# Three 512-column spin matmuls become 52 of 64 columns in the opening of a retention and Mish-MLP kernel

## The chip, the core and the metric

The kernel runs on one core of one Trainium2 chip. The metric is the device time of one execution, in microseconds (us). A core has a matrix engine (TensorE, "PE" in the profile; its weight loads are listed apart as "PEld"), a vector engine (VectorE, "DVE"), a scalar engine (ScalarE, "ACT"), GpSimd ("POOL") and SyncE ("SP"), which here only issues DMAs. Each engine works through its own list of instructions in order and waits on semaphores for the others.

## What is computed

A linear recurrence with decay (retention) over 4 batches, 8 heads, 768 steps and 64 channels, followed by a two-layer network over the 3072 tokens:

```python
for t in range(S):
    state = gamma * state + einsum('bhd,bhe->bhde', k[:, :, t], v[:, :, t])
    y[:, :, t] = scale * einsum('bhd,bhde->bhe', q[:, :, t], state)
x = y.transpose(0, 2, 1, 3).reshape(B * S, H * D)     # 3072 x 512
h = x @ w_in                                          # 512 x 2048
g = h * tanh(log1p(exp(h)))                           # Mish
out = g @ w_out                                       # 2048 x 512
```

Inputs and output are float32; the matrix work is done in float16 with float32 sums.

## The kernel before

The steps are cut into chunks of 128 (`C`). Within a chunk the outputs come from a masked matrix of scores (q times k, lower triangle) times v; across chunks a 64x64 state per head is carried. Chunks are gathered into blocks: the first block has four, the others two each (`BLOCKS`). For a block, the kernel makes the retention output transposed (`xt`), multiplies it by `w_in` (lines 687, 818, 1055), applies Mish on ScalarE, multiplies by `w_out` (lines 954, 1207, 1267) and stores. From the second block on, both products are done with seven half-size products in place of eight, which is where the many sums on VectorE come from. The order of instructions is written out by hand (`tc.manual_schedule()`); no scheduler moves them.

The change lies in `first_block`, before any data has arrived. SyncE issues the loads of the first 512 steps of q (`load_first_q`, tile `qfirst`), then of k and v, then of the weights. While they travel, GpSimd writes two constants, the identity `ident` (float16) and the triangle `tri` (float32), and TensorE runs matmuls whose result nobody reads ("spins"). There are two kinds: `spin_wide` (line 457) multiplies `tri` by copies of itself in float32, `n` times 128 columns, which the hardware does in two records of one instruction; `spin` (line 452) multiplies `ident` by copies of itself in float16, 512 columns a matmul. All write into the first score tile `at`, which the first scores overwrite later. In front of the first transpose stand two wide spins of 512 columns (`HP` is 4) and `spin(at, 8)`, two matmuls of 512 columns.

What follows on TensorE, in order: the transposes of the first half of q (line 264, eight of 128 columns, in `turn_first_q`), which need q scaled by VectorE (line 257); a wide spin of 128 columns; the eight transposes of the second half, whose input VectorE and GpSimd share; the transposes of k (line 307, `turn_two`), four for each half of the heads; a wide spin of 128; the scores (line 322). ScalarE copies the first transposed q out (line 272) and the transposed k (line 312); VectorE casts k (line 291), copies the second transposed q (line 274) and then masks the scores (line 329). The state sums (lines 341, 351, 353), the outputs (lines 382, 389) and the first product with `w_in` (line 1055) follow.

Of the kernel before, what the change touches and what calls it, by code (L numbers as in the profile page):

```python
# [16 lines left out]
def kernel(  # L17
# [9 lines left out]
    nc = tc.nc  # L27
# [6 lines left out]
    HP = H // 2  # L34
# [3 lines left out]
    HB = P // R  # L38
# [45 lines left out]
    ident = cpool.tile([P, P], FP16, name="ident")  # L84
# [158 lines left out]
    def load_first_q():  # L243

        qf = wstage.tile([P, H, CPB, D], FP32, name="qfirst", tag="wt", bufs=4)
        for a in range(0, H, H // 2):
            nc.sync.dma_start(
                qf[:, a:a + H // 2],
                q[0, a:a + H // 2, :TB].rearrange("h (p r) d -> p h r d", r=CPB))
        return qf  # L250

    def turn_first_q(qf, half, shared=False):
        a, n = half * (H // 2), H // 2
        q16 = castp.tile([P, CPB, n, D], FP16, name="qfirst16", bufs=1, tag=f"qfirst16_{half}")
        m = n // 2 if shared else n
        for b in range(0, n, m):
            (nc.gpsimd if b else nc.vector).tensor_tensor(
                q16[:, :, b:b + m].rearrange("p r h d -> p h r d"), qf[:, a + b:a + b + m],
                qs_spread[:, a + b:a + b + m].unsqueeze(3).broadcast_to((P, m, CPB, D)),
                op=ALU.mult)  # L260
        t_ps = mmps.tile([P, n // 2, CPB, P], FP16, name="t_ps", tag="mm")
        for i in range(n // 2):
            for r in range(CPB):
                nc.tensor.transpose(t_ps[:, i, r], q16[:, r, 2 * i:2 * i + 2], ident)  # L264
        return t_ps

    def first_q_out(half, t_ps, eng):
        n = HP // 2
        dst = qfirst_t[:, half * n:(half + 1) * n].rearrange("p i (t r) -> p i t r", r=CPB)
        src = t_ps.rearrange("p i r t -> p i t r")  # L270
        if eng is nc.scalar:
            nc.scalar.copy(dst, src)
        else:
            eng.tensor_copy(dst, src)

    def load_two(nm, s, half):
        t = lpool.tile([P, HP, R, D], FP32, name=nm + "f", tag=nm + "f", bufs=6 if nm == "v" else 4)
        nc.sync.dma_start(
            t, dict(k=k, v=v)[nm][
                0, half * HP:(half + 1) * HP, s * R * P:(s + 1) * R * P].rearrange(  # L280
                "h (p r) d -> p h r d", r=R))
        raw[nm, s, half] = t

    def cast_two(nm, s, half, by_vector=False):
        src = raw.pop((nm, s, half))
        if nm == "k":
            if s not in k16s:
                k16s[s] = castp.tile([P, 2, R, HP, D], FP16, name="qk16")
            dst = k16s[s][:, half].rearrange("p r h d -> p h r d")
            if by_vector:  # L290
                nc.vector.tensor_copy(dst, src)
            else:
                nc.scalar.copy(dst, src)
        else:
            v16s[s, half] = castp.tile([P, R, HP, D], FP16, name="v16")
            nc.gpsimd.tensor_tensor(
                v16s[s, half].rearrange("p r h d -> p h r d"), src,
                vs_two[:, half * HP:(half + 1) * HP].unsqueeze(3).broadcast_to((P, HP, R, D)),
                op=ALU.mult)
# [10 lines left out]
    def turned_two(s, half):  # L310
        n = HP // 2
        nc.scalar.copy(kts[s][:, half * n:(half + 1) * n], t16s.pop((s, half)))
# [133 lines left out]
    def at_tile():  # L446
        return atps.tile([P, 2, HP // 2, R, C], FP32, name="at", tag="at")

    def spin(at, n):
        for i in range(0, n, HP):  # L450
            m = min(HP, n - i)
            nc.tensor.matmul(
                at[:, 0].rearrange("p j r t -> p (j r) t")[:, :m], ident,
                ident.unsqueeze(1).broadcast_to((P, m, P)), start=True, stop=True)

    def spin_wide(at, n):
        nc.tensor.matmul(  # L457
            at[:, 0].rearrange("p j r t -> p (j r) t")[:, :n], tri,
            tri.unsqueeze(1).broadcast_to((P, n, C)), start=True, stop=True)
# [570 lines left out]
    def load_weights():  # L1030
        for s in range(NSL):
            load_w("in", s)
        for s in range(NSL):
            load_w("out", s)
        room(CPB)
        room(CPB + 1)
        load_one(CPB, 0, nc.sync)
        load_one(CPB, 2, nc.sync)
        load_one(CPB + 1, 0, nc.sync)
# [19 lines left out]
    def first_block():  # L1059
        qf = load_first_q()  # L1060
        for s in range(2):
            for nm in "kv":
                for half in range(2):
                    load_two(nm, s, half)
        nload[0] = CPB
        load_weights()
        xts[0] = xtp.tile([P, CPB, HP, C], FP16, name="xt")

        at = at_tile()
        spin_wide(at, HP)  # L1070
        spin_wide(at, HP)
        spin(at, 8)
        tq = turn_first_q(qf, 0)
        spin_wide(at, 1)
        first_q_out(0, tq, nc.scalar)
        tq = [tq, turn_first_q(qf, 1, True)]
        cast_two("k", 0, 0, True)
        turn_two(0, 0)
        turned_two(0, 0)
        cast_two("k", 0, 1, True)  # L1080
        turn_two(0, 1)
        first_q_out(1, tq[1], nc.vector)
        turned_two(0, 1)
        spin_wide(at, 1)
        scores_half(0, 0, at)
        mask_half(0, 0, at)
        for half in range(2):
            cast_two("v", 0, half)
        at = at_tile()
        spin_wide(at, 1)  # L1090
        scores_half(0, 1, at)
        mask_half(0, 1, at)
        cast_two("k", 1, 0)
        turn_two(1, 0)
        turned_two(1, 0)
        cast_two("k", 1, 1)
        outer_first(0)
        state_first(0)
        at = at_tile()
        scores_half(1, 0, at)  # L1100
        mask_half(1, 0, at)
        y = atps.tile([P, 2, HP, C], FP32, name="y_ps", tag="at")
        in_two = [y[:, c] for c in range(2)]
        present_first(0, in_two, range(HP))
        turn_two(1, 1)
        turned_two(1, 1)
        state_first(1)
        past_first(1, in_two)
        xt_out(0, y)
        for half in range(2):  # L1110
            cast_two("v", 1, half)
        cast_win(0, 0, nc.gpsimd)
        at = at_tile()
        scores_half(1, 1, at)
        mask_half(1, 1, at)
        y = [atps.tile([P, 2, HP, C], FP32, name="y_ps", tag="at")[:, 0] for _ in range(2)]
        outer_first(1, [0])
        state_first(2)
        h_ps = [mmps.tile([P, 1, TB], FP32, name="h_ps", tag="mm") for _ in range(2)]
        for u in range(2):  # L1120
            first_g1(h_ps[u], u, 0)
        present_first(1, y, range(HP))
        past_first(2, y)
        past_first(3, y)
        cast_win(0, 1, nc.vector)
        xt_out_by_two(2, y)
        for u in range(2, FPS):
            h_ps.append(mmps.tile([P, 1, TB], FP32, name="h_ps", tag="mm"))
            first_g1(h_ps[u], u, 0)
        for u in range(FPS):  # L1130
            first_g1(h_ps[u], u, 1)
            mish(0, u, h_ps[u])
        for s in range(1, NSL - 1):
            for half in range(2):
                cast_win(s, half, nc.vector)
            if s == 1:
                fourth_state()
            if s == 2:
                late.extend(win_sums(0))
                some_late(8)  # L1140
        room_for_sums()

        def more_sums():
            late.extend(win_sums(1))
            some_late(8)
            late.extend(weight_sums(0) + weight_sums(1))

        plan = {6: [(cast_win, NSL - 1, 0, nc.scalar)],
                7: [(cast_win, NSL - 1, 1, nc.scalar), (more_sums,)],
                9: [(cast_wout, 0, 1), (room_for_more,), (bring_first,)],  # L1150
                10: [(some_late, 1)],
                12: [(g_sum, 1)],
                13: [(cast_wout, 1, 2), (room_for_more,), (g_sum, 2), (g_sum, 3)],
                16: [(load_more,)]}
        for u in range(FPS, NFB):
            g1(0, u)
            for fn, *args in plan.get(u + 1, ()):
                fn(*args)
        first_g2()
        hsnaps.append(gp.tile([P, 4, TB], FP32, name="hsnap", tag="g0"))  # L1160
# [251 lines left out]
```

## Time and profile before

| | us |
|---|---|
| three timed runs | 192.44, 192.24, 191.39 |
| their median | 192.24 |
| the profiled execution | 191.71 |
| its span, first to last instruction | 189.8 |
| TensorE busy in it | 183.3 |
| VectorE, ScalarE, GpSimd busy in it | 156.7, 126.0, 94.7 |

The profile is one execution recorded by the hardware. Its span is shorter than its time, since start and end of the program lie around it. In its rows, "128x512 f32" is partitions by elements; "x8" counts instructions; "L264" is line 264 of the kernel. "[0.25 <-PE t_ps L264]" says that the engine had been idle for 0.25 us and what ended that. A merged row of the timeline gives the first start and the time covered, not the duration of one instruction. The end of a matmul is modelled, so the record of one overlaps the next; steps between starts are the better measure. The chain of waits starts at the last instruction and goes back, at each step, to what released it or to the instruction before it on its engine.

### The profile page before, as it was taken

The numbers are of one execution on the slowest core, as the hardware profiler recorded it, in microseconds if no ns is written. First come the engines' busy times: TensorE is split into PE (matmuls) and PEld (weight loads), VectorE is DVE, ScalarE is ACT, GpSimd is POOL, SyncE is SP. The second block draws the span as 40 slices with busy tenths as digits, with TensorE's granted clock in tenths as the row PEclk, the third lists the DMA queues.
The fourth block names the chain that finished last, engine by engine and source line by source line (L and its number), as shares of the span: only waits on it lengthen the run. The fifth ranks groups of instructions, "written<-read, shape, count | busy, mean of one in ns | idle before, by whom it ended". The sixth has DMA issues, their size and how long they took to land.

```text
span 189.8 us, 7746 instructions
## 1 busy us (share of the span) xinstructions
PE 183.3 (97%) x3298; PEld 156.9 (83%) x3298; DVE 156.7 (83%) x330; ACT 126.0 (66%) x244; POOL 94.7 (50%) x135
## 2 busy tenths in 40 slices
PE   6989999999999999999999999999999999999992
PEld 2667546875988988988988988988988988989981
DVE  3997899889899698797897897797897897796662
ACT  3362699463893983894883883983884974975960
POOL 6570205696767937934934935915925923000000
PEclk9999999999999999999999999999999999999999
DMA  4999999999999999999996996996997953300203
GB/s 165 351 369 406 405 406 279 269 217 147 186 195 281 193 264 217 175 192 170 176 184 148 159 176 196 207 233 40 196 205 106 155 152 60 114 3 12 102 0 111
DMA packets 95521, 36.17 MB, mean 191 GB/s; under 512 B 82560, under 2 KB 88960, under 8 KB 95488
## 3 DMA queue, kind: packets, MB, share of 16 engines
q1 hardware_dynamic: 74112, 32.78, 73.7%
q0 software_dynamic: 21088, 2.62, 21.7%
q8 instruction: 25, 0.41, 0.9%
q10 hardware_dynamic: 288, 0.30, 0.4%
q14 instruction: 8, 0.07, 0.1%
HBM read 27.30 MB, written 6.29 MB: 177 GB/s over the span
## 4 chain that ended last, share of the span: by engine, by line
PE 94%; DVE 3%; issue 1%; POOL 0%; ACT 0%; POOLq 0%; DVEq 0%
PE h_ps L818 34%; PE o_ps L954 32%; PE h_ps L687 6%; PE o_ps L1207 5%; PE at L457 2%; PE h_ps L1055 2%; PE o_ps L1267 2%; PE y_ps L542 2%; PE at L509 2%; PE u_ps L495 2%; DVE am L329 2%; PE y_ps L553 2%; PE t_ps L264 1%; DVE osb L975 1%; PE at L322 0%
## 5 line engine op out<-in xcount | busy, mean ns | idle before, releaser
L838 DVE TENSOR_TENSOR hsum<-h_ps,hsnap 128x512 f32<-128x512 f32 x60 | 38.6, 685 | 9.7 <-ACT hsnap L828 6.8
L828 ACT COPY hsnap<-h_ps 128x512 f32<-128x512 f32 x60 | 32.1, 589 | 10.0 <-PE h_ps L818 9.7
L818 PEld LDWEIGHTS <-wsum 128*128 128x128 f16 x640 | 36.2, 98 | 0.2
L833 ACT ACTIVATE g<-hsum 128x512 f16<-128x512 f32 x60 | 34.6, 642 | 0.6 <-DVE hsum L838 0.2
L954 PEld LDWEIGHTS <-gsum 128*128 128x128 f16 x320 | 30.4, 98 | 3.7
L818 PE MATMUL h_ps<-xsum,wsum 128*128 128x128 f16 x480 | 30.2, 219 | 0.0
L954 PE MATMUL o_ps<-tmat,gsum 128*128 128x256 f16 x240 | 29.5, 273 | 0.0
L818 PEld LDWEIGHTS <-win 128*128 128x128 f16 x480 | 28.2, 98 | 0.9
L426 POOL DMA_DIRECT2D qk<-in_k_dram x36 | 27.6, 781 | 0.0
L954 PEld LDWEIGHTS <-g 128*128 128x128 f16 x248 | 22.7, 98 | 2.5
L414 POOL TENSOR_TENSOR qk<-qf,qvs 128x512 f16<-128x512 f32 x20 | 21.5, 1077 | 0.2 <-issue 0.2
L431 POOL TENSOR_TENSOR v<-vf,qvs 128x512 f16<-128x512 f32 x20 | 21.2, 1085 | 0.0
L954 PE MATMUL o_ps<-wout,g 128*128 128x256 f16 (+1 forms) x168 | 20.8, 267 | 0.0
L818 PE MATMUL h_ps<-xt,win 128*128 128x128 f16 x320 | 19.6, 219 | 0.0
L603 POOL TENSOR_TENSOR stc<-suc,gcv 128x256 f16<-128x256 f32 x15 | 9.9, 663 | 15.7 <-DVE suc L598 15.7
L560 ACT COPY hsum<-y_ps 128x512 f32<-128x512 f32 x9 | 5.3, 585 | 18.4 <-PE y_ps L553 18.4
L975 DVE TENSOR_TENSOR osb<-o_ps,snap 128x256 f32<-128x256 f32 (+1 forms) x32 | 13.0, 413 | 5.0 <-PE o_ps L954 2.5
L439 POOL COPY gate<-gsum 128x1 f16<-128x1 f16 x10 | 1.8, 185 | 26.8 <-DVE gsum L925 26.8
L963 ACT COPY snap<-o_ps 128x256 f32<-128x256 f32 x31 | 11.4, 371 | 5.5 <-PE o_ps L954 5.3
L818 PE MATMUL h_ps<-xsum,win 128*128 128x128 f16 x160 | 12.3, 220 | 0.0
L818 PE MATMUL h_ps<-xt,wsum 128*128 128x128 f16 x160 | 12.2, 219 | 0.0
L833 ACT ACTIVATE g<-h_ps 128x512 f16<-128x512 f32 x20 | 12.0, 598 | 0.0
(142 smaller groups left out, 310.6 us busy)
## 6 DMA issues: line engine op xcount, KB each, us to landing
vf<-in_v_dram SPq DMA_DIRECT2D x24, 256.0 KB, 6.0
out_dram<-osb SPq DMA_DIRECT2D x22, 256.0 KB, 3.5
qf<-in_q_dram SPq DMA_DIRECT2D x20, 256.0 KB, 4.9
wi<-in_moe_w_in_dram SPq DMA_DIRECT2D x3, 1024.0 KB, 10.5
wt<-in_moe_w_out_dram SPq DMA_DIRECT2D x3, 1024.0 KB, 9.3
qk<-in_k_dram POOLq DMA_DIRECT2D x36, 64.0 KB, 4.7
qfirst<-in_q_dram SPq DMA_DIRECT2D x2, 512.0 KB, 4.3
kf<-in_k_dram SPq DMA_DIRECT2D x4, 256.0 KB, 5.0
```

What stands on the lines that cost most here:

```text
L414: nc.gpsimd.tensor_tensor(by_head(g, room16(g)[0]), by_head(0, loaded[g][0]), f.broadcast_to((P, 2, HP, D)), op=ALU.mult)
L426: nc.gpsimd.dma_start(room16(g)[1][:, x::2], src[:, HP * x:HP * x + HP])
L431: nc.gpsimd.tensor_tensor(room16(g)[2], loaded[g][2], vs.unsqueeze(2).broadcast_to((P, H, D)), op=ALU.mult)
L603: by.tensor_tensor(stcs[g], sus.pop(g), decay, op=ALU.mult)
L687: nc.tensor.matmul(h_ps[:, j], win(s, f, bp), xt(blk, bp), start=(bp == 0), stop=(bp == NBP - 1))
L818: nc.tensor.matmul(h_ps[g][:, f], w(g, f, d), x(d), start=first and f == 0 and d == 0, stop=d == n - 1, skip_group_check=True)
L828: nc.scalar.copy(x, h_ps)
L833: nc.scalar.activation(gt[:, fb:fb + FPS, j * P:(j + 1) * P], h, AF.Mish, scale=inv_boost3)
L838: nc.vector.tensor_tensor(h, h_ps, x, op=ALU.add)
L954: nc.tensor.matmul(t, x(f), w(f)[:, c], start=first and f == 0, stop=f == n - 1, skip_group_check=True)
L963: nc.scalar.copy(x[:, c], t)
L975: nc.vector.tensor_tensor(dst[:, c], t, plus[:, c], op=ALU.add)
```

## The change

The second wide spin and the two float16 spins are replaced by 52 matmuls of 64 columns, `ident` times its own first 64 columns. Each has its own load of `ident`. Three matmuls with their loads go (four records, as the wide one counts twice), 52 with theirs come, and all stand ahead of the first transpose on TensorE. No other engine's list changes.

```diff
+    def spin_narrow(at, n):
+        for i in range(n):
+            nc.tensor.matmul(
+                at[:, 0, 0, 0, :HB], ident, ident[:, :HB], start=True, stop=True)
...
         at = at_tile()
         spin_wide(at, HP)
-        spin_wide(at, HP)
-        spin(at, 8)
+        spin_narrow(at, 28)
+        spin_narrow(at, 24)
         tq = turn_first_q(qf, 0)
         spin_wide(at, 1)
         first_q_out(0, tq, nc.scalar)
```

`HB` is 64. The line numbers of the changed kernel are higher by five behind the new function: 457 becomes 462, 264 stays.

## The prediction

> **What bounds the kernel now.** I read the page first, then the chain of work that ended last, then the timeline of the opening. The page:
>
> ```profile
> span 189.8 us, 7746 instructions
> PE 183.3 (97%) x3298; PEld 156.9 (83%) x3298; DVE 156.7 (83%) x330; ACT 126.0 (66%) x244; POOL 94.7 (50%) x135
> PEclk9999999999999999999999999999999999999999
> ```
>
> TensorE (PE) is busy 97% of the span, so the kernel is bound by it wherever it has no reason to wait. The chain of waits shows where it has one (start, length, what; us):
>
> ```profile
> 1.87 3.78 PE at L457 x4
> 5.65 0.85 PE at L452 x2
> 6.50 0.85 PE t_ps L264 x8
> 7.36 0.53 PE at L457 x2
> 7.89 0.57 PE t_ps L264 x8
> 8.45 0.24 PE t_ps L307 x4
> 8.69 0.02 issue
> 8.71 0.59 ACT qkt L312
> ...
> 9.35 0.45 PE at L322 x16
> ...
> 9.89 0.73 DVE am L329
> ...
> 11.03 1.21 DVE am L329
> 12.25 0.60 DVE st L353
> 12.84 1.14 DVE am L329
> 13.98 0.04 issue
> 14.03 0.42 PE at L322 x16
> ...
> 185.30 1.19 DVE osb L975 x4
> ```
>
> Up to 8.7 us the chain is TensorE alone: the spins (L457, L452), then the transposes (L264, L307). From 8.71 to 14.0 it runs ACT, scores, and the masks of VectorE (L329), and from 14.03 nothing but TensorE until the closing additions at 185.30. Nothing later absorbs a delay: what reaches the mask at 9.89 late should come out at the end one for one, in both directions. So the change is decided between 3.7 and 9.9 us. The timeline there (start, length):
>
> ```profile
> 2.88 0.34 PEld L457 LDWEIGHTS at<-tri 128*128 128x128 f32 x1 [0.52 <-issue]
> 3.74 0.34 PEld L457 LDWEIGHTS at<-tri 128*128 128x128 f32 x1 [0.52 <-issue]
> 4.59 0.15 PEld L452 LDWEIGHTS <-ident 128*128 128x128 f16 x1 [0.52 <-issue]
> 4.69 2.02 DVE L257 TENSOR_TENSOR qfirst<-qfirst,qvs 128x1024 f16<-128x1024 f32 x2 [1.80 <-DMA qfirst<-in_q_dram]
> 5.44 0.15 PEld L452 LDWEIGHTS <-ident 128*128 128x128 f16 x1 [0.70 <-issue]
> 5.97 0.10 PEld L264 LDWEIGHTS <-qfirst 128*128 128x128 f16 x1 [0.37 <-DVE qfirst L257]
> 6.29 1.06 PE L264 MATMUL t_ps<-ident,qfirst 128*128 128x128 f16 x8
> 6.77 1.47 DVE L291 CAST qk<-kf 128x512 f16<-128x512 f32 x2
> 7.68 0.77 PE L264 MATMUL t_ps<-ident,qfirst 128*128 128x128 f16 x8
> 8.29 0.61 PE L307 MATMUL t_ps<-ident,qk 128*128 128x128 f16 x8
> 8.49 1.23 DVE L274 COPY qfirst_t<-t_ps 128x1024 f16<-128x1024 f16 x1 [0.25 <-PE t_ps L264]
> ```
>
> Each load starts as the matmul before it starts, so steps between loads are steps between matmuls: an fp32 record of 512 columns takes 0.85 us (2.88, 3.74, 4.59, 5.44), and a wide spin is two such records. The first transpose's load was released by VectorE at 5.97, but the transpose itself starts at 6.29, behind the spins: 0.32 us of spinning is already too long here.
>
> One more thing has to be read: TensorE's clock. The durations of one kind of instruction (min/median/max, ns):
>
> ```profile
> L264 PEld LDWEIGHTS <-qfirst x16: 98/151/151, 6.0 to 8.2; 128*128 128x128 f16 x16
> L264 PE MATMUL t_ps<-ident,qfirst x16: 219/314/314, 6.3 to 8.2; 128*128 128x128 f16 x16
> ```
>
> The first eight transposes have 314 ns each and cover 1.06 us, so they follow each other by (1.06 - 0.314)/7 = 0.107 us; the L307 ones cover 0.61 us and, at the 219 ns of the fast ones, step by (0.61 - 0.219)/7 = 0.056 us. TensorE runs at half speed until about 8.0 us, inside the second eight. The page's clock row has 9 in every slice and so doesn't show this first half speed; a table by stretches shows the reverse switch at the end (from:to, length, busy times of PE, PEld, DVE, ACT and POOL, clock, DMA, GB/s):
>
> ```profile
> 185.50:188.91 3.41, 0.66 (x12) 0.48 (x9) 0.99 (x4) 0.00 (x0) 0.00 (x0) 1.00 0.42 154
> 188.92:189.80 0.88, 0.00 (x0) 0.00 (x0) 0.00 (x0) 0.00 (x0) 0.00 (x0) 0.50 0.00 0
> ```
>
> TensorE ends at 185.50 + 0.66 = 186.2, and the clock is halved 2.7 us later: the clock follows how busy TensorE has been, with a delay of microseconds.
>
> **The change part by part.** Removed: one fp32 wide spin, two records, 2 x 0.85 = 1.71 us (3.73 to 5.44), and the two fp16 ones, 2 x 0.425 = 0.85 us (L452 in the chain). Added: 52 pairs of a load and a matmul of 64 columns. No row has a 128x128 load with 64 moving columns. From below: at half speed 512 columns take 0.425 us, so 64 take 0.053. From above: the cold transposes carry the same load and twice the columns and step by 0.107. The nearest row with 64 columns is this one:
>
> ```profile
> 39.34 0.32 PE L610 MATMUL u_ps<-v,qk 128*64 128x64 f16 x8
> ```
>
> Eight matmuls, two at a time in the two column halves, in four steps; a record of this kind lasts 196 ns at least, so first to last start is at most 0.12 us, 0.041 us a step at full clock, 0.082 at half. I take 0.053: in the transposes the load is hidden entirely, since cold and warm step by exactly their 128 columns (0.107, 0.056), and a 64-column step need only hide the same load behind half the time. 52 x 0.053 = 2.77 us. Sum on TensorE: 2.77 - 1.71 - 0.85 = +0.21 us; the first transpose starts at 6.50 instead of 6.29. At 0.107 it would be 5.56 - 2.56 = +3.0. Were the clock full from the start of the narrow ones, it would be about 1.5 us, below 2.56, but only the 0.32 us up to VectorE's release at 5.97 could be had there.
>
> What becomes of the 0.21: the second eight transposes start at 7.89 instead of 7.68. Before, four of them start by 8.0 and the rest at the full clock; now two do. Two transposes pass from 0.107 to 0.056, which gives back 0.10. L307 ends 0.11 later, ACT's copy starts at 8.82, the scores and the mask follow at 10.0, and the end moves by +0.11. VectorE's L274 shifts by the same (8.49 to 8.60, ending at 9.83), still ahead of the mask; its other input, the casts, ends at 8.24. No DMA is moved, and nothing on ACT, VectorE, GpSimd or SP's queue changes place.
>
> The code grows. The page's row for instruction loads:
>
> ```profile
> q8 instruction: 25, 0.41, 0.9%
> ```
>
> 25 packets, one per 16 KB, each 0.009 x 16 x 189.8 / 25 = 1.1 us of one DMA engine. Some 100 more instructions (52 pairs less the removed) shift where these loads fall; I cost that at nothing, because the load runs beside the work on the instructions already held, and in the chain TensorE has no piece that waits for one. Uncovered, one would cost up to 1.1 us.
>
> Two rules of the Trainium skill bear on this. "TensorE: Matmul & The Clock Gate", Part 1, says that the warm-up is a time of sustained activity, about 3.4 us in a free-running window, and not a number of matmuls. The trace agrees in kind: half speed to about 8.0 us, a drop at 188.9 with TensorE idle since 186.2; by that rule more, smaller matmuls neither hasten nor delay the switch, and the sum stays +0.11. The same page of the Trainium skill, Part 2, section "LDWEIGHTS (loading the stationary operand)", gives a load of 128 columns as 128/1.2 ns, an estimate of 107 ns, which speaks against this change: a 64-column matmul could not hide it, and the sum would be the +3.0 us bound at the first transpose. The warm transposes, at 0.056 us with a load each, contradict that figure at full clock; at half clock no row here decides.
>
> **The rivals.** *The clock turns earlier.* An fp32 record takes twice the time per column of an fp16 one (0.85 against 0.425). If the switch counts columns, full-rate work begins at 3.73 instead of 5.44 and the turn could come 1.7 us sooner, at 6.3. For it: 3.6 us of spinning from 1.87 had not turned the clock by 5.44. Against: nothing in one execution tells columns from mere time. The transposes would shrink at once, but VectorE caps the gain: L291 ends at 8.24, L274 takes 1.23, so the mask can start at 9.53 at best instead of 9.89. That is -0.36: 191.35.
>
> *The clock turns later* (this ends slower). If 64-column matmuls with a load between count for less than a 512-column stream, the switch at 8.0 is missed. The place: the seven transposes, four of L307, the next spin and the scores between 8.0 and 9.9 run at half speed. Ten steps x 0.051 + 0.095 of longer drain + 0.1 (the shift above) + about 0.25 for the scores (L322's 0.45 would at most double; the next spin hides behind ACT's copy): the mask starts near 10.85, +0.95. From there to 14 the masks hide TensorE, but after 14 each microsecond at half speed costs half a one. Turning by 14: 192.7. At 18: 2 more, 194.7. At 20.2, when TensorE has been busy for the 6.1 us that it took from 1.87: 195.8. I price it at 193.7. For it: the chain between 8.7 and 14 leaves TensorE waiting for ACT and the masks, so a missed switch isn't soon made up. Against: a pair without a gap keeps the array as busy as now. It decides when the step of a pair exceeds its columns by enough.
>
> *The load isn't hidden.* At 0.082 a pair, 4.26 us from 3.73: the first transpose at 8.0, now at full clock; eight, the spin (0.27), eight, and the three up to the fourth of L307 end at 8.0 + 0.45 + 0.27 + 0.45 + 0.17 + 0.22 = 9.56 instead of 8.69, +0.87. At 0.107: 9.29 at the first transpose, +2.15. So 192.6 to 193.9; middle 193.2. The load figure of the Trainium skill, named above, would give the upper value.
>
> *A code load lands late:* +1.1 at one page, 192.8 or more.
>
> **How the numbers follow.** The sum stands on the profiled execution, 191.71 us. The three timed runs have 192.44, 192.24 and 191.39, median 192.24; the profiled one is 0.53 below that. The opening explains part of such a spread: the switch at 8.0 need not fall at the same place each time, and from the cap of VectorE (-0.36) to a missed one (+0.95) the same kernel could take 191.35 to 192.7. So I lay the +0.11 on the mean of all four, 191.95, and predict 192.1.
>
> Chances: the sum as worked out 0.47; clock earlier 0.18; clock later 0.22; load not hidden 0.10; code load 0.03. A measurement of this kernel can tell about 0.5% (1 us) from no change. Faster by more takes a median below 191.28: of the earlier clock 0.11 (the -0.36 lies at that edge when set against a median of 192.24) and 0.01 of the sum's scatter, 0.12 in all. Slower by more takes one above 193.2: 0.20 of the later clock, 0.09 of the unhidden load, 0.03 of the code load, 0.02 of the scatter, 0.34. The rest, 0.54, is no change. The likeliest case alone spans 191.4 to 192.6. The range reaches down to 191.2 for the earlier clock and up to 193.9, the dearest unhidden load and about half of the later clock; what is left out is the other half and a little below, under 0.2.
>
> **What would show it.** In the changed profile: narrow matmuls stepping by 0.053 us from 3.73, the first transpose at 6.50, transposes passing from 314 to 219 ns at about the same time as now, ACT's L312 at 8.8, the mask at 10.0, TensorE unbroken from about 14.1. Narrow steps of 0.08 or 0.107 prove the load. Transposes already at 219 ns in the first eight show the earlier clock, L307 or L322 still long the later one. I am wrong if the end moves while the mask's start doesn't, since then the time went somewhere after 14 us.

## The result, and the profile after

The changed kernel takes 193.36 us in the median of 22 runs (192.57 to 194.62), the kernel before 192.25 in the median of 22 runs beside them (191.39 to 193.93). The ratio is 1.0053, with an interval of 1.0033 to 1.0073: slower by about 1 us. The profiled execution took 192.85 us, with a span of 191.1, against 191.71 and 189.8 before. Three lines of the page after:

```profile
span 191.1 us, 7842 instructions
PE 183.4 (96%) x3346; PEld 158.6 (83%) x3346; DVE 156.6 (82%) x330; ACT 126.1 (66%) x244; POOL 94.7 (50%) x135
q8 instruction: 26, 0.43, 0.9%
```

TensorE's busy time is the same as before to 0.1 us; the span is 1.3 us longer. So the loss is waiting, not work. There is one more code load than before (26 against 25). First the opening, in the chain of waits of the kernel after (start, length, what):

```profile
3.95 2.77 PE at L458 x52
...
8.85 0.60 ACT qkt L312
...
10.03 0.73 DVE am L329
...
14.17 0.42 PE at L322 x16
...
186.59 1.19 DVE osb L980 x4
```

52 pairs in 2.77 us are 0.0533 us each. The mask (L329) starts at 10.03, 0.14 after its old 9.89, and the scores of L322 at 14.17, 0.14 after 14.03. The closing additions start at 186.59, 1.29 after 185.30. So 1.29 - 0.14 = 1.15 us were lost after 14 us. The timeline of the opening after confirms the first part:

```profile
3.74 2.98 PE L458 MATMUL at<-ident 128*128 128x64 f16 x52
6.54 1.04 PE L264 MATMUL t_ps<-ident,qfirst 128*128 128x128 f16 x8
7.90 0.69 PE L264 MATMUL t_ps<-ident,qfirst 128*128 128x128 f16 x8
```

The first transpose starts at 6.54 instead of 6.29, and the second eight at 7.90. Where the rest went, the later chain of the kernel after shows:

```profile
49.19 1.05 POOL qk L414
50.24 0.02 issue
50.26 5.63 DMA qkt<-qk
55.89 0.04 issue
55.93 0.32 PE at L514 x16
```

GpSimd scales q and k of a chunk (L414), a DMA transposes them (`turn_by_dma`, issued by SP), and TensorE multiplies the result into scores (L514; line 509 before). That DMA took 5.63 us. Its counterpart before was issued at 50.20 and landed at 54.48, 4.29 us later, 0.05 us ahead of the matmul that needed it at 54.53. The views of DMAs say the same, before and after (the last number is the time from issue to landing):

```profile
qkt<-qk SPq DMA_TRANSPOSE x1, 4.3
```

```profile
qkt<-qk SPq DMA_TRANSPOSE x1, 5.6
```

Matching the instructions of the two traces one by one, TensorE is late by 0.05 to 0.14 us from 14 us up to here; this matmul is late by 55.93 - 54.53 = 1.40, and what follows by 1.2 to 1.3 to the end. The wait has a line of its own among TensorE's waits (in total, times, longest), which before has no line for this cause:

```profile
PE at L514 <- DMA qkt<-qk: 1.2, 1, 1.2
```

What the traffic did meanwhile is seen in a table by stretches (from:to, length, busy times of PE, PEld, DVE, ACT and POOL, clock, DMA, GB/s). Before:

```profile
51.00:51.50 0.50, 0.50 (x13) 0.50 (x11) 0.12 (x1) 0.50 (x3) 0.50 (x1) 1.00 1.28 291
...
52.00:52.50 0.50, 0.50 (x11) 0.41 (x9) 0.50 (x2) 0.50 (x2) 0.50 (x1) 1.00 1.50 153
52.50:53.00 0.50, 0.50 (x12) 0.50 (x11) 0.50 (x2) 0.50 (x2) 0.50 (x2) 1.00 1.57 156
```

The same after, to the end of the wait, and a row of its view of DMA queues from 50.3 to 52.3 us:

```profile
51.00:51.50 0.50, 0.50 (x13) 0.50 (x11) 0.18 (x1) 0.50 (x2) 0.50 (x1) 1.00 0.04 9
...
52.00:52.50 0.50, 0.50 (x11) 0.41 (x8) 0.50 (x2) 0.50 (x2) 0.50 (x1) 1.00 3.92 31
52.50:53.00 0.50, 0.50 (x11) 0.50 (x10) 0.50 (x2) 0.50 (x2) 0.50 (x2) 1.00 0.11 3
...
55.00:56.00 1.00, 0.07 (x8) 0.07 (x12) 0.96 (x4) 0.75 (x2) 0.28 (x1) 1.00 1.28 285
```

```profile
q8 instruction: 1, 0.02, 3.3%
```

The traffic falls away twice, to 9 GB/s at 51.0 and to 31 and 3 from 52 to 53, where before it ran at 291, 153 and 156; from 55 on TensorE stands still until the data are there. And in this window TensorE's queue for code (q8) fetched 16 KB: the records put it at 50.71, lasting 1.05 us. Before, the nearest such loads were at 47.70 and 56.14, on either side of the flight. The transpose also took SP longer to issue, in the timelines before and after:

```profile
50.20 1.25 SPq L443 DMA_TRANSPOSE qkt<-qk  x1
```

```profile
50.26 2.04 SPq L443 DMA_TRANSPOSE qkt<-qk  x1
```

So the theory for the experiments was: the 98 instructions shift the points at which code is fetched, and a fetch that falls into the flight of this DMA makes TensorE wait. The rivals: the longer spins (0.21 us) start everything later and collide with something; or the clock.

### The profile page after: what moved, and what is told of

It is laid out like the page before. It is cut to its first block, busy times and chain, and to the rows that moved or that the text cites. A ratio compares the mean times of both kernels' runs of the same rounds, so it can differ in the third digit from the quotient of the medians.

```text
span 191.1 us, 7842 instructions
## 1 busy us (share of the span) xinstructions
PE 183.4 (96%) x3346; PEld 158.6 (83%) x3346; DVE 156.6 (82%) x330; ACT 126.1 (66%) x244; POOL 94.7 (50%) x135
## 3 DMA queue, kind: packets, MB, share of 16 engines
HBM read 27.30 MB, written 6.29 MB: 176 GB/s over the span
## 4 chain that ended last, share of the span: by engine, by line
PE 87%; DVE 6%; DMA 3%; POOL 1%; issue 1%; ACT 0%; POOLq 0%; DVEq 0%
PE o_ps L959 32%; PE h_ps L823 30%; PE h_ps L692 5%; PE o_ps L1212 5%; DMA qkt<-qk 3%; PE h_ps L1060 2%; PE y_ps L547 2%; PE at L514 2%; DVE am L329 2%; PE u_ps L500 1%; PE y_ps L558 1%; PE at L458 1%; PE at L462 1%; DVE am L580 1%; PE t_ps L264 1%
## 5 line engine op out<-in xcount | busy, mean ns | idle before, releaser
L414 POOL TENSOR_TENSOR qk<-qf,qvs 128x512 f16<-128x512 f32 x20 | 21.5, 1076 | 0.2 <-issue 0.2
```

Source lines behind the costliest of these rows:

```text
L414: nc.gpsimd.tensor_tensor(by_head(g, room16(g)[0]), by_head(0, loaded[g][0]), f.broadcast_to((P, 2, HP, D)), op=ALU.mult)
```

## The experiments

Each kernel was timed in five rounds (12 runs) beside the kernel before. "+91" counts the entries that TensorE's list has more than before, waits and the like included, so the kernel after has +99. All replace the same three spins by `n` matmuls of `w` columns of a helper `spin_narrow(at, n, w)`, like the one in the change, unless said otherwise. Line numbers are as after.

**Count without time, time without count, and half the count.** The first kernel keeps the count nearly and the old length of the spins (48 x 0.0533 = 2.56 us), the second keeps the old instructions and adds 256 columns (0.21 us), the third has the old length in 24 matmuls of 128 columns.

```diff
+        spin_narrow(at, 48, HB)                        # first
...
         spin(at, 8)
+        spin(at, 2)                                    # second
...
+        spin_narrow(at, 24, P)                         # third
```

> The spin time of before (48 pairs of 64 columns, 48 x 0.053 = 2.56 us, against 2.56) with 91 more instructions on TensorE. Theory 'place of the code': the 16 KB code load that lay at 50.7 us in the changed kernel lies there again within some 0.3 us, inside the DMA transpose issued at 50.3; scores L509 wait about 1.2 us for it and the kernel is some 1.0 us slower than before. Rival 'time': the first transpose starts at 6.29 again, and without the delay of the opening the kernel takes what before takes, within 0.2 us, with no wait of TensorE for a DMA.

> The spins of before and one more of 256 columns (0.21 us, 2 instructions): the opening of the changed kernel without its instructions. Theory 'place of the code': code loads where before has them (47.7 and 56.1 us), no wait of TensorE for the DMA transpose, +0.1 us at most. Rival 'time': the first transpose at 6.50, everything behind it 0.11 later, and the end about 1.0 us slower as in the changed kernel.

> The spin time of before (24 pairs of 128 columns) with 43 more instructions. Theory 'place of the code': the load moves by some 40 instructions only, to between 50.7 and 56.1 us; if it falls before about 54 us, inside the transpose's flight, the kernel is about 1 us slower, if later it is as before. Rival 'time': as before within 0.2 us. A third reading, that narrow matmuls themselves cost something (clock), expects half of the changed kernel's loss, 0.5 us.

The count alone (+91) is slower: 194.2 us, ratio 1.0064 [1.0033, 1.0095]. The time alone (+2) is not: 192.59, 0.9992 [0.9955, 1.0028]. Half the count (+43) is not either: 191.85, 0.9965 [0.9932, 0.9997]. That parts the count from the time: the narrow matmuls' extra 0.21 us is worth nothing measurable, and their number is what costs.

The traces agree in kind. Code was fetched at 51.97 us in the first kernel, not between 48 and 56 in the second, at 53.32 in the third, in the last microsecond of a flight that took 4.10 us; in the first it took 4.92. The exact place was missed: for the first kernel a load within 0.3 us of 50.7 and a wait of about 1.2 us were expected, and it was 1.3 us later, with a wait of 0.5.

The first kernel lost more elsewhere, though. Two of TensorE's waits in it, and its chain of waits from 11 to 18 us:

```profile
PE h_ps L1060 <- POOL win L212: 0.9, 1, 0.9
PE at L514 <- DMA qkt<-qk: 0.5, 1, 0.5
```

```profile
8.44 6.28 DMA wi<-in_moe_w_in_dram
...
14.77 1.05 POOL win L212
15.86 1.05 PE h_ps L1060 x8
```

Its first code load came at 12.12, while the first part of `w_in` was landing: 15 of that DMA's 16 parts were there at 13.45, the last at 14.71, 1.26 us later. Before, with no load of code in that flight, they were at 13.41 and 13.43; it is the third part of `w_in`, in flight at the code load of 14.60, that had 17.38 and 18.61. So one sixteenth of a load can land late when code is fetched during its flight. In the kernel as changed, whose first code load is at 13.06, the first part is whole at 13.53 and the second has the late sixteenth (14.88 and 16.17), for which TensorE shows no wait: this cost is absent.

**More instructions: a whole page of 256, and 151.** If the position of the code loads alone decides, a shift by 255 should restore the old positions, and one by 151 move the load out of the flight.

```diff
+        spin_narrow(at, 130, 24)                       # a page, +255
...
+        spin_narrow(at, 78, 40)                        # +151
```

> 130 pairs of 24 columns, 255 more instructions, one code load of 256 within one. Theory 'place of the code': the loads lie at the same work as before, one number further (about 47.7 and 56.1 us plus the delay of the opening), the transpose issued at about 50.3 lands undisturbed and the kernel takes what before takes plus what the spins are longer; at 0.020 us a pair that is nothing, at a floor of 0.027 a pair 0.9 us on the spins. Rival 'number of instructions' (each instruction costs): 2.5 times the changed kernel's loss, about 2.5 us slower.

> 78 pairs of 40 columns: the spin time of before (78 x 0.033 = 2.6 us), 151 more instructions. Theory 'place of the code': the load that lay at 50.7 us with 99 more comes some 52 instructions earlier, near 48 us, before the transpose of 50.3 is issued; scores L509 wait less than 0.4 us and that part of the loss is gone. The first load comes near 11.5 us, into the saturated opening, and can hold back a sixteenth of the load it meets by about 1.2 us (w_in, as with 91 more: 14.71 instead of 13.45); where its user has no slack the first product L1055 is late by up to 0.8. So 0 to 0.8 us slower than before, all of it ahead of 20 us. Rival 'each instruction costs': 151/99 of the changed kernel's loss, 1.5 us or more, with the loss at L509.

Neither came out as expected. The whole page is slower: 194.32 us, 1.0070 [1.0036, 1.0103]. Its timeline and its waits:

```profile
3.74 3.58 PE L458 MATMUL at<-ident 128*128 128x24 f16 x130
7.17 0.61 PE L264 MATMUL t_ps<-ident,qfirst 128*128 128x128 f16 x8
```

```profile
PE at L514 <- DMA qkt<-qk: 1.4, 1, 1.4
PE t_ps L307 <- ACT qk L293: 1.2, 1, 1.2
PE h_ps L1060 <- issue: 1.1, 1, 1.1
```

The pairs took 3.58 us, so the first transpose came 0.88 us late, and the first load of code came already at 8.58, among the loads of k: the part of k that L293 casts had 15 of its 16 parts at 9.79 and the last at 11.12. Later loads of code fell at 17.50, 23.50, 40.25 and 50.35. The last of these lies in the flight of the transpose before ours, from 46.23 to 52.44 (6.21 us; 15 of its 16 parts had landed at 51.01); ours followed it from 52.77 to 57.81, 5.04 us with no load of code inside. So here the wait at L514 is not explained by a load in its own flight, and the restored order was not reached. The chain of waits shows why ours was issued so late:

```profile
46.62 6.01 DMA qk<-in_k_dram
...
52.77 5.04 DMA qkt<-qk
```

It waited for a load of k that was in flight at the same code load: 15 of its parts were there at 51.52, the last at 52.63. GpSimd's scaling, the other input, ended at 51.96, so up to 0.7 us of the wait of 1.4 comes from that late part; why the flight itself took 5.04 us is not shown. Nor is it shown what ended the wait on "issue" at L1060, which began 0.4 us after the code load of 17.50 had ended. The 151 gave 192.93 us, 1.0031 [1.0002, 1.0060], with a wait at L514 of 0.8 us where less than 0.4 was expected: the load fell at 51.23, not near 48. The positions don't move in proportion to the count (51.23 at +151, and 50.71 in the profile at +99), and I could not place them by counting.

**The transpose 1 us earlier.** If the wait comes of missing slack, an earlier issue should remove it. In `steps_of_first`, GpSimd's cast of q goes ahead of its gate; done to the kernel after, to the kernel before, and to the one with 24 matmuls.

```diff
-            "at1": [(gate_x, blk), (cast_q, a - 1), (bring_k, a)],
+            "at1": [(cast_q, a - 1), (gate_x, blk), (bring_k, a)],
```

> The changed kernel, with one step moved on GpSimd: the scaling of chunk 7's q ahead of its gate, so that the DMA transpose can be issued about 1 us earlier (49.2 instead of 50.3). Theory 'place of the code': the code load still falls into the transpose's flight (near 50.7), but the landing comes about 1 us sooner and L509 waits 0.3 us or less; the kernel is about 0.8 to 1.0 us faster than the changed one, so equal to before within 0.3 us. Rival 'the loss is elsewhere': the wait at L509 shrinks but the end doesn't move, about 1 us slower than before.

> The same step moved in the kernel of before. Theory 'place of the code': no code load falls into that transpose in the usual execution, which landed just in time, so the median gains 0.3 us at most, from the executions in which it lands late. If moving the step is a gain of its own (about 1 us here too), the experiment on the changed kernel says nothing about the code load.

> 24 pairs of 128 columns (43 more instructions) and the step moved. Theory 'place of the code': with 43 more the load fell at 53.3, at the very end of the transpose's flight, and cost 0.3 us; landing 1 us earlier takes that away: 0.2 to 0.8 us faster than before. Rival: equal to the run with 43 more alone (0.7 us faster than before).

On the kernel after: 192.89 us, 1.0033 [1.0007, 1.0060]. The transpose ran from 49.56 to 54.55, with code fetched at 52.31. It still took 5.00 us: 15 of its 16 parts were there at 53.03, the last at 54.55. Its wait at L514 is gone, as expected, but the time is not: a kernel equal to before within 0.3 us was expected, and it is 0.8 us slower than the 192.08 of before beside it. Two waits of other kinds stand in the list instead:

```profile
PE h_ps L1060 <- POOL win L212: 0.7, 1, 0.7
PE h_ps L823 <- DVE hsum L843: 0.4, 1, 0.4
```

The first goes with another load of code, at 11.83: the first part of `w_in` had 15 of its parts at 13.50 and the last at 14.62, as in the kernel with +91. The second belongs to the move: the kernel before with the same move shows it too (0.4), without a wait at the scores, at 192.38 us, 1.0010 [0.9983, 1.0037]. The one with 24 matmuls and the move came to 192.05, 0.9996 [0.9972, 1.0019], and its transpose, with no load of code inside, took 2.72 us; 0.2 to 0.8 us faster than before was expected of it and missed. With the move in both, the change costs 1.0033 / 1.0010 = 1.0023; without it, 1.0053. The direction is that of the theory, but the intervals overlap, so at the end of the kernel this stays unsettled.

**Steps between, and repeats.** Two counts between 0 and 91 that keep the length of the spins, the 24 matmuls again, and the kernel after again.

```diff
+        spin(at, 6)                                    # +35
+        spin_narrow(at, 18, P)
...
+        spin_narrow(at, 36, 84)                        # +67
```

> 20 float16 spins of mixed width: the spin time of before, 35 more instructions. Theory 'place of the code': the load lies near 53.9, when the transpose is landing; no wait above 0.3 us, equal to the run with 43 more within 0.3 us, and not slower than before.

> 36 pairs of 84 columns: the spin time of before, 67 more instructions. Between 43 more (load at 53.3 us, no loss) and 91 more (52.0, loss): the load is expected near 52.5, inside the transpose's flight. Theory 'place of the code': a wait at L509 of 0.3 to 1.2 us, 0.3 to 1.0 us slower than the run with 43 more on this chip. Rival 'each instruction costs': a third of the way between 43 and 99 more.

> 24 pairs of 128 columns (43 more instructions) a second time: whether it is really faster than before. Theory 'place of the code': the profile shows the load near 53.3 and a wait at L509 of 0.3 us or less; 0 to 0.7 us faster than before, and 1.0 to 1.6 us faster than the changed kernel on this chip. If it comes out slower than before, its first result was chance.

> The changed kernel unchanged, on the same chip as the next three, for a second profile. Theory 'place of the code', in two places: a load in the flight of chunk 7's transpose with a wait at L509 of 0.5 to 1.3 us in this execution too; and, if the first code load falls before about 13.0 us, the first part of w_in lands 1.2 us late and L1055 loses 0.6. 0.5 to 1.0% slower than before. Rival 'chance meeting': no wait at L509 in this execution.

| instructions more | code load near the flight | transpose, issue to landing | wait at L514 | ratio to before |
|---|---|---|---|---|
| 0 (before) | 47.70, 56.14 | 50.20 to 54.48, 4.29 | none | 1 |
| +2 | 47.74, 56.29 | 50.34 to 54.26, 3.92 | none | 0.9992 [0.9955, 1.0028] |
| +35 | 53.39 | 50.18 to 54.24, 4.06 | none | 1.0000 [0.9969, 1.0031] |
| +43 | 53.32 | 50.20 to 54.30, 4.10 | 0.3 | 0.9965 [0.9932, 0.9997] |
| +43 again | 54.02 | 50.22 to 54.15, 3.93 | none | 0.9989 [0.9960, 1.0017] |
| +67 | 52.18 | 50.16 to 55.46, 5.30 | 0.9 | 1.0046 [1.0017, 1.0075] |
| +91 | 51.97 | 50.88 to 55.80, 4.92 | 0.5 | 1.0064 [1.0033, 1.0095] |
| +99 (after) | 50.71 | 50.26 to 55.89, 5.63 | 1.2 | 1.0053 [1.0033, 1.0073] |
| +99 again | 51.67 | 50.74 to 55.49, 4.76 | 0.2 | 1.0052 [1.0024, 1.0079] |
| +151 | 51.23 | 50.60 to 55.80, 5.20 | 0.8 | 1.0031 [1.0002, 1.0060] |
| +255 | 50.35 | 52.77 to 57.81, 5.04 | 1.4 | 1.0070 [1.0036, 1.0103] |

(The ratios are of twelve or more runs, the other columns of one profiled execution each. The kernels with the moved step are left out.)

The ratio steps up between +43 and +67, where the code load moves from the last microsecond of the flight into its middle. All six kernels at +67 and above are slower with an interval clear of 1, counting the repeat; none of the four below is. The repeat of the kernel after is as slow as the first time, but its profile missed its expectation: the wait at L514 is 0.2, where 0.5 to 1.3 was expected. Its chain of waits, and two of its waits on TensorE, show why:

```profile
40.15 6.32 DMA qk<-in_k_dram
46.46 0.04 issue
46.51 0.34 PE u_ps L500 x15
```

```profile
PE u_ps L500 <- issue: 0.6, 1, 0.6
PE u_ps L500 <- DMA qk<-in_k_dram: 0.6, 1, 0.6
```

A load of code at 44.17 fell into the load of k instead: 15 of its parts were there at 45.14, the last at 46.46. TensorE was 0.71 late behind it, which gave the transpose that much cover. So the same loss is paid at another place when the code load lies elsewhere. The wait on "issue" came at 74.85, amid like instructions, after a load of code at 73.24; TensorE waited for nothing that the profile shows.

**The same transposes with and without a load of code.** The kernel has 18 transposes by DMA, and the 14 profiles (before, after and the twelve experiments) have the code loads at different places in them. At six of the 18, little else disturbs the flight (at least two profiles have it under 2.82 us), and there the same transpose can be compared between kernels; two of these 84 flights have no landing on record:

| issued near, us | flight with a load of code begun 0.1 to 2.3 us after issue | flight with none from 0.7 us before issue to 2.3 after |
|---|---|---|
| 75 | 9 flights, 3.78 to 5.13 | 5 flights, 2.75 to 2.77 |
| 102 | 9 flights, 3.26 to 4.29 | 2 flights, 2.77 and 2.78 |
| 116 | 1 flight, 3.67 | 10 flights, 2.76 to 2.78 |
| 145 | 11 flights, 2.89 to 4.54 | 1 flight, 2.77 |
| 151 | 3 flights, 3.02 to 3.17 | 6 flights, 2.74 to 2.75 |
| 159 | 3 flights, 2.95 to 3.81 | 9 flights, 2.72 to 2.74 |

The two columns nowhere overlap: 36 flights take 2.89 us or more, 33 take 2.78 or less. The later the load begins within these 2.3 us, the longer the flight (at 145 us: 2.89 with a load 0.10 after issue, 4.17 at 1.15, 4.54 at 1.64). Thirteen flights with a load from 0.7 us ahead of the issue to 0.1 behind it are mixed, 2.74 to 3.30. Before has such long flights too (3.44 at 102 us, 4.54 at 144), and no wait of TensorE for them: there is slack. At the other twelve places flights last from 2.7 to 7.3 us, and no such order was found.

## Why the prediction was wrong

The working of the opening held. A narrow step is 0.0533 us (0.053 predicted), the first transpose started at 6.54 (6.50), ACT's copy at 8.85 (8.82), the mask at 10.03 (10.0). The load of the weights was hidden, and even pairs of 24 columns took (7.17 - 3.74) / 130 = 0.026 us each; the rival that the load shows is refuted. The clock neither lagged nor hurt: after 8 us the second eight transposes ran as before.

The step that failed is "I cost that at nothing", said of the shift of the code loads. It was costed at nothing "because the load runs beside the work on the instructions already held". That reason looks at TensorE as the reader of its code. The runs show another cost: data DMAs that are in flight beside a load of code land late, and TensorE then waits for the data, 1.2 us at L514. The size was named (up to 1.1 us; measured 1.15 after 14 us), as a rival of chance 0.03; its mechanism, code that reaches TensorE late, is not what the profile of the changed kernel shows. Of all loads of code in the kernel the prediction asked only whether TensorE waits for one, and not which DMA with no slack would next share the engines with one. It was there to find in the trace of before: this transpose landed 0.05 us ahead of its use, in a flight between two loads of code.

"Nothing later absorbs a delay" held for this loss: it reached the end nearly whole, 1.40 at 55.93 and 1.29 at 186.59. That 193.36 lies between the stated 191.2 and 193.9 is luck: the upper part was there for the unhidden load and the later clock, and neither occurred. A further part of the distance from 192.1 is the base: the sum stood on 191.95, and the kernel before measured 192.25. For the 0.14 of the opening no run shows a price: 0.21 us more of spinning alone gave 0.9992.

The rival of the earlier clock fell for a reason of its own. In the profile of the kernel with 0.21 us more of spinning the clock turned early, so that the first transposes started at 6.03 and the later ones were short, and still the matmul that started at 10.50 before was only 0.01 earlier: TensorE then waits 0.2 us at L307 for ScalarE's cast of k (L293). The prediction had put the cap at VectorE and a gain of 0.36 under it. So the spread of the runs, too, was ascribed to the clock without a run that bears it out.

The prediction's own test, "I am wrong if the end moves while the mask's start doesn't, since then the time went somewhere after 14 us", met exactly this case but for the 0.14.

What is shown: the number of instructions ahead of the first transpose costs the time and their duration doesn't, and the time is lost where TensorE waits for a DMA (L514, or L500 for k, or L1060 for `w_in`). That the load of code is what makes the DMA late is read from the records. For loads of k and of `w_in`, one part of sixteen is 1.3 us late. For this transpose the flight is longer in the five profiles of the table at +67 to +151 (4.76 to 5.63 us against 3.92 to 4.29 in the five at +43 and below), though it was long at +255 (5.04) without one. For transposes at six quieter places the two groups of flights don't overlap. It is not shown that no part of the loss is code reaching TensorE late: three waits on "issue" (1.1 us at +255, 0.6 at +99 again, 0.3 at +91) begin 0.4 to 1.1 us after a load of code ended; in the profile of the changed kernel there is none. An experiment that moves a load of code and nothing else was not tried, nor one for these waits. No kernel was found that beats the one before: 24 matmuls of 128 columns gave 0.9965 once and 0.9989 [0.9960, 1.0017] again.

## What to carry to other kernels

Instructions added to an engine can cost more than their own time, by the place to which they push every later fetch of code; list those fetches (here one of 16 KB at irregular steps of 4 to 18 us) beside the DMAs in flight and ask which of them has no slack at its user. A few tenths of a per cent that appear far from an edit, with the same busy times, are looked for in a wait on a DMA that was just in time before. Then run one variant with the count and without the time, and one the other way round, before believing either.

## What the runs showed of the hardware

A load of code took 0.9 to 1.5 us in nearly all records, and three DMAs of data that were in flight had one of their 16 parts land 1.3 us after the other 15 (13.45 and 14.71; 9.79 and 11.12; 45.14 and 46.46). Over the 14 profiles, leaving out the transposes, the last part comes over 0.8 us behind the fifteenth in 267 of 1017 DMAs with a load of code in flight up to then, and in 11 of 635 without. The Trainium skill, "Runtime: NRT & Kernel Launch", section "Instruction fetch mechanics", says that code is refilled in blocks of 16 KiB and that crossing a block is mostly hidden. The traces agree on the block (26 packets, 0.43 MB). On hidden they differ: in the kernels from +67 on the shift of the blocks goes with a loss of 0.3 to 0.7%, at waits for data of up to 1.4 us.

Around this transpose the traffic of all 16 engines falls away, not that of one. The kernel with +67, and the one with +43 (first run), GB/s from 49.4 to 56 us in 40 slices of 0.165 us:

```profile
GB/s 286 292 287 290 233 81 8 0 0 0 0 6 202 280 171 119 228 150 147 147 150 136 53 25 3 8 9 9 9 9 203 215 156 150 158 168 255 278 279 280
```

```profile
GB/s 287 290 285 296 289 146 26 0 0 0 0 0 150 289 223 126 130 138 149 157 157 152 171 241 171 97 74 88 145 156 171 193 220 245 254 261 271 258 251 238
```

Both stop near 50.5 to 51.3, with no load of code near; before has such a stop too, at 49.4 to 49.9. The first stop is thus no sign of a code load. The second one goes with a load: with +67 the traffic is at most 25 GB/s for seven slices, 1.2 us, from 53.2 on, some 1 us after the code load at 52.18; with +43 it never falls under 74 there. In this second phase, the kernel after falls to 3 GB/s (52.5 to 53), the one before has 90 at the lowest. The others of the table agree but for one: the lowest slice of this phase has 2, 9 and 28 GB/s at +91, +99 again and +151, and 80, 63 and 84 at +2, +35 and +43 again; at +255, with no load in the flight, a slice falls to 26 all the same. How one engine's 16 KB stop the other 15 was not found out. SP's issue of this transpose took 1.24 to 1.36 us, but 2.04 after and 2.17 with +151, where a code load began 0.45 and 0.63 us into it; where one began 0.93 and 1.09 us into it (+99 again, +91) it took 1.24 and 1.26.
